# Transposed x in one tile per supergroup, and another pace of the x loads, in an attention and MLP kernel

## Chip, cores and metric

The kernel runs on 1 core of one Trainium2 chip. The metric is the device time of one execution in microseconds (us); the median over runs counts. Below, PE is TensorE, ACT ScalarE, DVE VectorE, POOL GpSimd and SP SyncE. POOL and SP issue the DMAs here; each issues in the order of its own queue, so an issue that waits holds back all that stand behind it.

## The reference

Four batches of 12480 tokens with 128 channels pass through an attention with 32 inducing points, and the result through an MLP of width 2048 with a leaky activation.

```python
def _attn_ref(x, inducing):            # x (4, 12480, 128), inducing (32, 128)
    def mab(q, kv):
        s = scale * (q @ kv.transpose(0, 2, 1))
        s = s - s.max(-1, keepdims=True)
        a = np.exp(s)
        a /= a.sum(-1, keepdims=True) + 1e-09
        return a @ kv
    h = mab(I, x)                      # 32 rows per batch
    return mab(x, h)

def _moe_ref(x, w_in, w_out, alpha):   # w_in (128, 2048), w_out (2048, 128)
    h = x @ w_in
    g = np.maximum(h, 0.0) + alpha * np.minimum(h, 0.0)
    return g @ w_out
```

Each batch therefore needs its x twice: once in full for `h`, and then again for the scores of each token against `h`. Nothing of a batch's second half can start before all of its x has been seen.

## The kernel before

**Tiling.** A batch is six supergroups of 2048 tokens and a rest of 192. A supergroup is four groups of 512 tokens, so a batch has 25 groups (the last one is the rest), and groups are numbered through: batch 0 has 0 to 24, batch 1 has 25 to 49, and so on. A full group is worked in four slots, j 0 to 3; the rest in two. (g, j) below names a slot. There are 392 slots.

**One slot.** `fill` multiplies the softmax numerators of the group (`rep`, the 32 rows of a group copied to four blocks of partitions) by `hW` (which is `h` times `w_in`): four matmuls that write four of six PSUM banks (`ring`). ACT and DVE empty these banks through a ReLU into `gt`; a planner (`make_plan`, a beam search over estimated costs) decides beforehand which of the two takes which bank. After the fill come the tasks that are registered for the slot, then up to two POOL "moves", and then `mm2` of the slot before: four matmuls `acc<-gt,W` with `w_out` scaled by one minus alpha. The linear part of the activation is added by small matmuls (`hA`). In slots with a task that writes 32 output columns per matmul (scores and sums), `mm2` is written as 16 narrow matmuls in place of four wide ones.

**Output.** From the second supergroup of batch 0 on, the result comes out with channels on partitions. `turn` transposes 32x32 blocks on DVE into `yT`; the last group of a supergroup appends 20 moves: 16 shuffles `yq<-yT` (DMAs issued by POOL), and four times a multiplication by the reciprocal of the softmax denominators (`ob`, on POOL) with the DMA of the result. Two moves go out per slot, four at the end of the last batch.

**x.** For batch 0 a prologue loads and transposes x with PE. For the batches 1 to 3 this is done beside the slots of the batch before:

- `a_load` (POOL): 2048 tokens from DRAM into `xn`, cast to bf16, seven such tiles in rotation; the rest goes to `xnr`. The load is made to wait for the ACT instruction last recorded, so that it does not start before its slot.
- `a_xpose` (SP): a DMA transpose `xT<-xn`, one group later.
- `a_scores`: PE multiplies the inducing points by `xT`, ACT takes the exponential `e1`, SP transposes that by DMA into `e1T`.
- `a_accum`: PE multiplies `e1T` by `xn`; DVE adds the result to `hacc`.
- When all seven pieces are in, `h_sum`, `h_den`, `h_transpose`, `h_weights` and `h_linear` make `h`, `hW` and `hA`.
- `b_scores(s)`: PE multiplies `h` by `xT` of supergroup s, ACT takes the exponential, SP writes it to DRAM (`e2d<-e`). One group later `b_rep` reads it back with four SP DMAs (`rep<-e2d`), one for each block of 32 partitions. `b_den` makes the reciprocal of the denominators.

`xT` is one tile for a whole batch, in two buffers that alternate.

**Order.** Each instruction recorded through `pin` keeps its place in the program on its engine. `at(slot, fn, j)` registers a task; the loop from line 818 gives the groups. For each batch it registers first the `b_scores` and `b_rep` of its supergroups, and then the x work for the batch after it; where two tasks share a slot, the one registered first goes first. For the first supergroup of batch 1, `b_scores` stands in slot (21, 1) and `b_rep` in (22, 0); its first fill is in (25, 0). For the batches 2 and 3 the same two come one group earlier before the change of batch. For the rest of batch 0, `b_scores` is in (18, 3) and `b_rep` in (19, 3).

The tuples in the x part (lines 832 to 846) hold, for the seven pieces in the order 0, 1, rest, 2, 3, 4, 5, the group of the load (`k`), of the scores (`t`) and, as a distance from `t`, of the sum (`d`).

Of the kernel before, what the change touches and what calls it, by code (L numbers as in the profile page):

```python
# [16 lines left out]
P = 128  # L17
NB = 4
GRP = P * NB
NQ = 4  # L20
# [5 lines left out]
def kernel(  # L26
# [11 lines left out]
    bf16 = mybir.dt.bfloat16  # L38

    B, N, C = x.shape  # L40
# [3 lines left out]
    NS = N // SUP  # L44
    REM = N - NS * SUP
    JR = 2
    PR = REM // JR
    assert REM == PR * JR and 0 < PR <= 96 and PR % 16 == 0, REM
    NG = NS * NQ + 1
# [22 lines left out]
    const = ctx.enter_context(tc.tile_pool(name="const", bufs=1))  # L72
    work = ctx.enter_context(tc.tile_pool(name="work", bufs=2))
    xn_pool = ctx.enter_context(tc.tile_pool(name="xnp", bufs=7))
    xt_pool = ctx.enter_context(tc.tile_pool(name="xtp", bufs=2))
    gt_pool = ctx.enter_context(tc.tile_pool(name="gtp", bufs=4))
    head_pool = ctx.enter_context(tc.tile_pool(name="headp", bufs=3))
    rep_pool = ctx.enter_context(tc.tile_pool(name="repp", bufs=3))
# [21 lines left out]
    def mm(o, lhsT, rhs, start=True, stop=True, **kw):  # L100
        return pin(nc.tensor.matmul(o, lhsT, rhs, start=start, stop=stop, **kw))  # L101
# [5 lines left out]
    def new_batch(b):  # L107
        st = Batch()
        st.b = b
        st.xT = xt_pool.tile([C, NS, NQ, GRP], bf16, name="xT", tag="xT")  # L110
        st.xTr = xt_pool.tile([C, JR, PR], bf16, name="xTr", tag="xTr")
        st.xn = {}
        st.e1T = {}
        st.sc = scale
        st.rs = None
        st.e2 = {}
        st.d = {}
        st.rep = {}
        st.rden = {}
        st.yT = {}  # L120
        if b > 0:
            st.es = work.tile([P, NS + 1], f32, name="es", tag="es")
            st.hacc = work.tile([P, C], f32, name="hacc", tag="hacc")
            nc.vector.memset(st.es[:], 0.0)
            nc.vector.memset(st.hacc[:], 0.0)
        return st

    def a_load(st, u, pieces=1):
        t0 = u * SUP
# [26 lines left out]

    def a_xpose(st, u):
        xn = st.xn[u]
        if u < NS:
            pin(nc.sync.dma_start_transpose(  # L160
                out=st.xT[:, u, :, :].rearrange("c q (j p) -> c (q j) p", j=NB),
                in_=xn[:].rearrange("p q f -> p (q f)"),
            ))
        else:
            pin(nc.sync.dma_start_transpose(
                out=st.xTr[:], in_=xn[:].rearrange("p j c -> p (j c)")
            ))


    def p_xpose(st, u, i, last=False):  # L170
        xn = st.xn[u]
        if u == NS:
            tp = bank()[:].bitcast(bf16)
            for j in range(JR):
                pin(nc.tensor.transpose(
                    tp[:, j * PR : (j + 1) * PR], xn[:, j, :], ident[:PR, :PR]
                ))
            pin(nc.vector.tensor_copy(
                out=st.xTr[:].rearrange("c j p -> c (j p)"), in_=tp[:, :REM]
            ))  # L180
            return
        cut = 2 if last else 1
        for h in range(cut):
            tp = bank()[:].bitcast(bf16)
            qs = range(2 * i + h * 2 // cut, 2 * i + (h + 1) * 2 // cut)
            for n, q in enumerate(qs):
                for j in range(NB):
                    k = n * NB + j
                    pin(nc.tensor.transpose(  # L189
                        tp[:, k * P : (k + 1) * P], xn[:, q, j * C : (j + 1) * C], ident[:]  # L190
                    ))
            dst = st.xT[:, u, qs[0] : qs[-1] + 1, :].rearrange("c q t -> c (q t)")
            w = len(qs) * GRP
            if h == 0:
                pin(nc.vector.tensor_copy(out=dst, in_=tp[:, :w]))  # L195
            else:
                pin(nc.scalar.copy(out=dst, in_=tp[:, :w]))

    def p_blocks(st, u, i):
        if u == NS:  # L200
            return [(st.xTr[:, j, :], st.xn[u][:, j, :]) for j in range(JR)]
        return [
            (st.xT[:, u, q, j * P : (j + 1) * P], st.xn[u][:, q, j * C : (j + 1) * C])
            for q in (2 * i, 2 * i + 1) for j in range(NB)
        ]

# [32 lines left out]
    def warm(st, n=1, a=0):  # L239
        for _ in range(n):  # L240
            mm(
                accs[a][:, 1:, :].rearrange("p k c -> p (k c)"), ident[:],
                st.xT[:, 0, 0, : 3 * P], start=False, stop=False, skip_group_check=True,
            )

    def p_sums(st):
# [33 lines left out]
    def a_scores(st, u):  # L280
        ps = bank()
        if u < NS:
            for q in range(NQ):
                mm(ps[32 * q : 32 * q + 32, :], IT[:], st.xT[:, u, q, :])
            e1 = e1_pool.tile([P, GRP], bf16, name="e1", tag="e1")
            pin(nc.scalar.activation(  # L286
                out=e1[:], in_=ps[:], func=EXP, scale=scale, accum_out=st.es[:, u : u + 1]
            ))
            e1T = e1_pool.tile([P, NB, P], bf16, name="e1T", tag="e1T")
            pin(nc.sync.dma_start_transpose(out=e1T[:], in_=e1[:]))  # L290
        else:
            mm(ps[0:M, :REM], IT[:], st.xTr[:].rearrange("c j p -> c (j p)"))
            pin(nc.scalar.activation(
                out=e1r[:, :, :PR],
                in_=ps[0:M, :REM].rearrange("m (j p) -> m j p", j=JR),
                func=EXP, scale=scale, accum_out=st.es[0:M, u : u + 1],
            ))
            e1T = work.tile([P, JR, M], bf16, name="e1Tr", tag="e1Tr")
            pin(nc.sync.dma_start_transpose(
                out=e1T[:], in_=e1r[:].rearrange("m j p -> m (j p)")  # L300
            ))
        st.e1T[u] = e1T
# [69 lines left out]
    def b_scores(st, s):  # L372
        ps = bank()
        if s < NS:
            for q in range(NQ):
                mm(ps[32 * q : 32 * q + 32, :], st.hT, st.xT[:, s, q, :])
            e2 = work.tile([P, GRP], bf16, name="e2", tag="e2")
            pin(nc.scalar.activation(out=e2[:], in_=ps[:], func=EXP, scale=scale_of(st)))  # L378
            w = GRP
        else:  # L380
            mm(ps[0:M, :REM], st.hT, st.xTr[:].rearrange("c j p -> c (j p)"))
            e2 = work.tile([M, REM], bf16, name="e2r", tag="e2r")
            pin(nc.scalar.activation(out=e2[:], in_=ps[0:M, :REM], func=EXP, scale=scale_of(st, M)))
            w = REM

        nq = NQ if s < NS else 1
        st.d[s] = dram.tile([32 * nq, w], bf16, name="e2d", tag="e2d" if s < NS else "e2dr")
        pin(nc.sync.dma_start(out=st.d[s][:], in_=e2[:]))
        st.e2[s] = e2
# [11 lines left out]
    def b_scores_pe(st, q):  # L401
        if q == 0:
            st.rep0 = rep_pool.tile([P, NQ, GRP], bf16, name="rep", tag="rep")
        ps = bank()
        mm(ps[:], st.hT4[:], st.xT[:, 0, q, :])
        pin(nc.scalar.activation(
            out=st.rep0[:, q, :], in_=ps[:], func=EXP, scale=scale_of(st)
        ))
        st.rep[q] = st.rep0[:, q, :]
# [254 lines left out]
    order = [0, 1, NS] + list(range(2, NS))  # L664
    st = new_batch(0)
# [94 lines left out]

    pool = accs[0][:, 0, :M]
    den = accs[1][:, 0, 0:1]
    halves = [(u, i) for u in order for i in range(1 if u == NS else 2)]
    n = len(halves)
    p_xpose(st, *halves[0])
# [30 lines left out]
    states = {0: st}  # L796
# [4 lines left out]
    def at(slot, fn, j=1, cost=None, narrow=False):  # L801
        tasks.setdefault((slot, j), []).append((fn, cost))
        if narrow:
            narrows.add((slot, j))
# [10 lines left out]
    at(2, late_finish, 0)  # L815
    at(2, lambda: linear(st, [1]), 0)

    for b in range(B):
        base = b * NG
        for s in range(1, NS + 1):  # L820
# [5 lines left out]
        if b + 1 < B:  # L826
# [3 lines left out]
                states[n] = new_batch(n)  # L830

            for i, u in enumerate(order):
                if b == 0:
                    k, t = (1, 3, 4, 6, 8, 10, 12)[i], (6, 7, 9, 11, 13, 15, 17)[i]
                    d = (4, 4, 4, 4, 4, 3, 2)[i]
                    turn_at = k + 1, 1
                else:
                    k, t = base + (-8, -6, -4, -3, 0, 3, 6)[i], base + (-3, -1, 1, 3, 6, 9, 12)[i]
                    d = (4, 5, 4, 5, 5, 4, 5)[i]
                    turn_at = k + 1, 1 if k + 1 == base - 1 else 3  # L840
                if i == 0:
                    at(k, begin)
                at(k, lambda n=n, u=u: a_load(states[n], u), 3 if i == b == 0 else 1)
                at(turn_at[0], lambda n=n, u=u: a_xpose(states[n], u), turn_at[1])
                at(t, lambda n=n, u=u: a_scores(states[n], u), 0, (215, "A", 680), narrow=True)
                at(t + d, lambda n=n, u=u: a_accum(states[n], u), 3, (200, "D", 220), narrow=True)
            k = base + NG - (6 if b == 0 else 7)
            at(k, lambda n=n: h_sum(states[n]), 0)
            at(k, lambda n=n: h_den(states[n]), 1, (250, "D", 500))
# [126 lines left out]
```

## Time and profile before

| | us |
|---|---|
| median of 11 runs | 587.93 |
| lowest and highest of them | 585.61, 593.45 |
| the profiled execution | 583.84 |
| its span in the profile | 582.1 |
| PE busy | 567.1 |
| ACT busy | 511.5 |
| DVE busy | 507.0 |
| POOL busy (its DMA issues counted) | 358.3 |

The median is that of whole executions. The span is the time from the first to the last instruction in the profile, and lies inside the profiled execution's own time. Busy times are sums over the span; a matmul's end is modelled, so PE's busy time holds some waiting. The views used below are: the page (busy times, the chain of work that ended last, DMA issues with the median time from issue to landing), the timelines of one engine (start, time taken, engine, line, operation, count, and in brackets the idle time before it with what ended it), and the waits (engine and line, what it waited for, total us, times, longest).

```text
PE   4999999999999999999999999999999999999997
POOL 6631056385674758775756576687674876766761
DMA  9959699977899499555799869854353454444333
```

These three rows cut the span into 40 slices of 14.6 us; a digit is the busy share in tenths. The last ten slices or so belong to the last batch, which has no x to load for a next one.

### The profile page before, as it was taken

The page shows a single profiled execution, that of the slowest core. Times are in us where ns is not written, and L with a number is a line of the kernel's source. Part 1 is how long each engine was busy: PE and PEld are TensorE (multiplying, and loading weights), DVE is VectorE, ACT ScalarE, POOL GpSimd, SP SyncE. Part 2 cuts the span into 40 slices and gives each one's busy share as a digit, 9 for nine tenths or more (in the row PEclk, how much of TensorE's full clock was granted, in tenths as well). Part 3 has the DMA queues.
Part 4 walks back from the last instruction along what each step waited for, and adds up shares of the span by engine and source line. Part 5 has one row for each costly group of instructions (what it writes and reads, how often), then busy time and mean ns, then how long its engine had stood idle before and what let it go on. Part 6 is the DMA issues. An engine that isn't in the chain of part 4 may idle for free.

```text
span 582.1 us, 14829 instructions
## 1 busy us (share of the span) xinstructions
PE 567.1 (97%) x5491; PEld 224.6 (39%) x5491; DVE 507.0 (87%) x851; ACT 511.5 (88%) x1010; POOL 358.3 (62%) x614
## 2 busy tenths in 40 slices
PE   4999999999999999999999999999999999999997
PEld 4675333333333333333333333333333333333375
DVE  3689998888988998898898989889899999999995
ACT  2588999998889999998989989999898999999986
POOL 6631056385674758775756576687674876766761
PEclk9999999999999999999999999999999999999999
DMA  9959699977899499555799869854353454444333
GB/s 198 216 108 205 119 178 196 186 160 145 171 240 196 122 200 217 160 163 111 165 193 211 182 136 218 177 149 149 99 155 114 131 127 140 128 113 141 112 107 135
DMA packets 94104, 92.75 MB, mean 159 GB/s; under 512 B 61984, under 2 KB 77520, under 8 KB 94032
## 3 DMA queue, kind: packets, MB, share of 16 engines
q0 software_dynamic: 24016, 60.29, 43.6%
q1 hardware_dynamic: 69872, 30.99, 25.5%
q8 instruction: 43, 0.70, 0.6%
q10 hardware_dynamic: 144, 0.52, 0.3%
q14 instruction: 29, 0.24, 0.2%
HBM read 40.20 MB, written 28.75 MB: 118 GB/s over the span
## 4 chain that ended last, share of the span: by engine, by line
PE 91%; ACT 3%; DMA 2%; DVE 2%; issue 1%; SPq 0%; DVEq 0%
PE acc L101 62%; PE ring L101 28%; ACT gt L485 3%; PE ring L189 1%; DVE gt L487 1%; DMA rep<-e2d 1%; DMA ind_f<-in_inducing_dram 1%; DMA e2d<-e 1%; DVE xT L195 0%; DVE rdt L424 0%; SPq L396 0%; DVE xn L757 0%; ACT e L378 0%; SPq L669 0%; DVE ind_b L707 0%
## 5 line engine op out<-in xcount | busy, mean ns | idle before, releaser
L485 ACT ACTIVATE gt<-ring 128x512 bf16<-128x512 f32 (+1 forms) x921 | 480.2, 600 | 50.3 <-ACT gt L485 28.1
L487 DVE TENSOR_SCALAR gt<-ring 128x512 bf16<-128x512 f32 x647 | 418.3, 682 | 51.7 <-PE ring L101 41.8
L101 PE MATMUL acc<-gt,W 128*32 128x512 bf16 (+2 forms) x2272 | 370.6, 377 | 0.0
L631 POOL DMA_DIRECT2D yq<-yT x352 | 173.3, 500 | 70.5 <-DMA xn<-in_x_dram 27.2
L101 PEld LDWEIGHTS <-W 128*128 128x128 bf16 (+1 forms) x2272 | 122.3, 97 | 147.6 <-issue 63.0
L101 PE MATMUL ring<-rep,hW 32*128 32x512 bf16 (+1 forms) x1600 | 165.3, 378 | 0.5 <-DMA rep<-e2d 0.2
L638 POOL TENSOR_TENSOR ob<-yq,rd 128x512 f32<-128x512 f32 x88 | 92.7, 1055 | 59.4 <-DMA yq<-yT 58.0
L101 PEld LDWEIGHTS <-hW 32*128 32x128 bf16 x1600 | 44.2, 91 | 158.1 <-issue 151.4
L649 POOL DMA_DIRECT2D out_dram<-ob x84 | 49.2, 585 | 27.9 <-POOL ob L638 24.6
L622 DVE STREAM_TRANSPOSE yT<-acc 128x512 f32<-128x512 f32 x88 | 62.3, 708 | 4.6 <-PE acc L101 4.6
L135 POOL DMA_DIRECT2D xn<-in_x_dram x28 | 15.8, 567 | 34.8 <-ACT gt L485 30.6
L101 PE MATMUL acc<-W,gt 128*128 128x128 bf16 (+1 forms) x544 | 36.1, 220 | 0.0
L101 PEld LDWEIGHTS <-gt 128*128 128x128 bf16 (+1 forms) x544 | 30.7, 99 | 5.7 <-issue 5.1
L101 PE MATMUL acc<-rep,hA 32*128 32x512 bf16 (+1 forms) x91 | 17.4, 371 | 0.0
L214 ACT ACTIVATE e1t<-ring 128x256 bf16<-128x256 f32 (+1 forms) x13 | 4.8, 372 | 10.6 <-PE ring L101 10.5
L195 DVE COPY xT<-ring 128x1024 bf16<-128x1024 bf16 (+1 forms) x12 | 7.9, 669 | 5.0 <-PE ring L189 4.6
L378 ACT ACTIVATE e<-ring 128x512 bf16<-128x512 f32 x18 | 11.0, 614 | 0.0
L286 ACT ACTIVATE e<-ring 128x512 bf16<-128x512 f32 x18 | 10.9, 603 | 0.0
L101 PE MATMUL ring<-xT,hT 128*32 128x512 bf16 (+1 forms) x98 | 10.3, 387 | 0.4
L189 PE MATMUL ring<-ident,xn 128*128 128x128 bf16 x96 | 8.8, 249 | 0.9 <-DVE xn L757 0.9
L593 POOL DMA_DIRECT2D out_dram<-obe x4 | 2.2, 548 | 11.7 <-DVE obe L580 11.7
L101 PEld LDWEIGHTS <-hT 128*32 128x32 bf16 (+1 forms) x122 | 4.6, 93 | 11.2 <-issue 10.7
(102 smaller groups left out, 160.3 us busy)
## 6 DMA issues: line engine op xcount, KB each, us to landing
yq<-yT POOLq DMA_DIRECT2D x352, 64.0 KB, 3.4
out_dram<-ob POOLq DMA_DIRECT2D x84, 256.0 KB, 2.9
rep<-e2d SPq DMA_DIRECT2D x92, 128.0 KB, 3.5
xn<-in_x_dram POOLq DMA_DIRECT2D x18, 512.0 KB, 6.8
e2d<-e SPq DMA_DIRECT2D x24, 128.0 KB, 3.1
xn<-in_x_dram POOLq DMA_DIRECT2D x10, 256.0 KB, 8.5
w_out_f<-in_moe_w_out_dram POOLq DMA_DIRECT2D x4, 256.0 KB, 11.2
out_dram<-obe POOLq DMA_DIRECT2D x4, 256.0 KB, 5.7
```

The costliest lines, as they stand in the source:

```text
L101: return pin(nc.tensor.matmul(o, lhsT, rhs, start=start, stop=stop, **kw))
L135: bi = pin(nc.gpsimd.dma_start(out=xn[:, i * w : (i + 1) * w, :], in_=src[:, i * w : (i + 1) * w, :]))
L189: pin(nc.tensor.transpose(tp[:, k * P : (k + 1) * P], xn[:, q, j * C : (j + 1) * C], ident[:]))
L195: pin(nc.vector.tensor_copy(out=dst, in_=tp[:, :w]))
L286: pin(nc.scalar.activation(out=e1[:], in_=ps[:], func=EXP, scale=scale, accum_out=st.es[:, u : u + 1]))
L378: pin(nc.scalar.activation(out=e2[:], in_=ps[:], func=EXP, scale=scale_of(st)))
L485: pin(nc.scalar.activation(out=gt[:, r, :w], in_=ps[:, :w], func=RELU))
L487: pin(nc.vector.tensor_relu(gt[:, r, :w], ps[:, :w]))
L622: pin(nc.vector.transpose(out=yT[:, :, q, :, :].rearrange("p a j c -> p j a c"), in_=acc[:].rearrange("p j (a c) -> p j a c", a=4),))
L631: pin(nc.gpsimd.dma_start(out=yq[32 * a : 32 * a + 32, k], in_=yT[32 * k : 32 * k + 32, a]))
L638: pin(nc.gpsimd.tensor_tensor(out=ob[:].rearrange("p j (k c) -> p j k c", k=4), in0=yq[:, :, q].rearrange("p k j c -> p j k c"), in1=bass. ...
L649: pin((nc.sync if ending else nc.gpsimd).dma_start(out=out[t0 : t0 + SUP, :].rearrange("(p q j) c -> q p j c", q=NQ, j=NB)[q], in_=ob[:],))
```

## The change

Three things change. The transposed x becomes one tile per supergroup, of which twelve rotate (24 KB per partition and batch before, the same bytes after), and the rest's tile gets three buffers; a tile is now taken when its transpose is issued (`new_xT` in `a_xpose`), not when the batch begins. The places of loads, scores and sums come from a table `PACE` with one row for each batch, counted from the batch's first group; the sum's place is now given itself and not as a distance. And for batch 1 the transposes move from j 1 to j 3 of their group.

```diff
-    xt_pool = ctx.enter_context(tc.tile_pool(name="xtp", bufs=2))
+    xt_pool = ctx.enter_context(tc.tile_pool(name="xtp", bufs=12))
...
-        st.xT = xt_pool.tile([C, NS, NQ, GRP], bf16, name="xT", tag="xT")
-        st.xTr = xt_pool.tile([C, JR, PR], bf16, name="xTr", tag="xTr")
+        st.xT = {}
...
+    def new_xT(st, u):
+        if u < NS:
+            st.xT[u] = xt_pool.tile([C, NQ, GRP], bf16, name="xT", tag="xT")
+        else:
+            st.xTr = xt_pool.tile([C, JR, PR], bf16, name="xTr", tag="xTr", bufs=3)
...
     def a_xpose(st, u):
         xn = st.xn[u]
+        new_xT(st, u)
...
-                mm(ps[32 * q : 32 * q + 32, :], st.hT, st.xT[:, s, q, :])
+                mm(ps[32 * q : 32 * q + 32, :], st.hT, st.xT[s][:, q, :])
...
+    PACE = [
+        [(1, 3, 4, 6, 8, 10, 12), (6, 7, 9, 11, 13, 15, 17), (10, 11, 13, 15, 17, 18, 19)],
+        [(-12, -9, -8, -6, -3, 0, 4), (-6, -3, -1, 0, 3, 7, 11), (0, 1, 4, 5, 8, 12, 16)],
+        [(-17, -13, -12, -9, -5, -1, 4), (-11, -7, -5, -3, 1, 5, 11), (-8, -4, 0, 1, 5, 9, 16)],
+    ]
     for b in range(B):
         base = b * NG
...
             for i, u in enumerate(order):
-                if b == 0:
-                    k, t = (1, 3, 4, 6, 8, 10, 12)[i], (6, 7, 9, 11, 13, 15, 17)[i]
-                    d = (4, 4, 4, 4, 4, 3, 2)[i]
-                    turn_at = k + 1, 1
-                else:
-                    k, t = base + (-8, -6, -4, -3, 0, 3, 6)[i], base + (-3, -1, 1, 3, 6, 9, 12)[i]
-                    d = (4, 5, 4, 5, 5, 4, 5)[i]
-                    turn_at = k + 1, 1 if k + 1 == base - 1 else 3
+                k, t, d = (base + v[i] for v in PACE[b])
+                turn_at = k + 1, 1 if (k + 1) % NG == NG - 1 else 3
...
-                at(t + d, lambda n=n, u=u: a_accum(states[n], u), 3, (200, "D", 220), narrow=True)
+                at(d, lambda n=n, u=u: a_accum(states[n], u), 3, (200, "D", 220), narrow=True)
```

Row b of `PACE` is for the loads of batch b + 1. In group numbers, the loads of batch 2 were posted in the groups 17, 19, 21 (rest), 22, 25, 28 and 31, and are now posted in 13, 16, 17 (rest), 19, 22, 25 and 29. Those of batch 3 were in 42, 44, 46 (rest), 47, 50, 53 and 56, and are now in 33, 37, 38 (rest), 41, 45, 49 and 54. Those of batch 1 stay where they were. All are posted at j 1, but for the very first, at j 3.

More of the change, by code (lines that the diff above doesn't have):

```diff
@@ L158, in a_xpose @@
         xn = st.xn[u]
+        new_xT(st, u)
         if u < NS:
             pin(nc.sync.dma_start_transpose(
-                out=st.xT[:, u, :, :].rearrange("c q (j p) -> c (q j) p", j=NB),
+                out=st.xT[u][:].rearrange("c q (j p) -> c (q j) p", j=NB),
                 in_=xn[:].rearrange("p q f -> p (q f)"),
@@ L191, in p_xpose @@
                     ))
-            dst = st.xT[:, u, qs[0] : qs[-1] + 1, :].rearrange("c q t -> c (q t)")
+            dst = st.xT[u][:, qs[0] : qs[-1] + 1, :].rearrange("c q t -> c (q t)")
             w = len(qs) * GRP
@@ L202, in p_blocks @@
         return [
-            (st.xT[:, u, q, j * P : (j + 1) * P], st.xn[u][:, q, j * C : (j + 1) * C])
+            (st.xT[u][:, q, j * P : (j + 1) * P], st.xn[u][:, q, j * C : (j + 1) * C])
             for q in (2 * i, 2 * i + 1) for j in range(NB)
@@ L242, in warm @@
                 accs[a][:, 1:, :].rearrange("p k c -> p (k c)"), ident[:],
-                st.xT[:, 0, 0, : 3 * P], start=False, stop=False, skip_group_check=True,
+                st.xT[0][:, 0, : 3 * P], start=False, stop=False, skip_group_check=True,
             )
@@ L283, in a_scores @@
             for q in range(NQ):
-                mm(ps[32 * q : 32 * q + 32, :], IT[:], st.xT[:, u, q, :])
+                mm(ps[32 * q : 32 * q + 32, :], IT[:], st.xT[u][:, q, :])
             e1 = e1_pool.tile([P, GRP], bf16, name="e1", tag="e1")
@@ L404, in b_scores_pe @@
         ps = bank()
-        mm(ps[:], st.hT4[:], st.xT[:, 0, q, :])
+        mm(ps[:], st.hT4[:], st.xT[0][:, q, :])
         pin(nc.scalar.activation(
@@ L762 @@
     den = accs[1][:, 0, 0:1]
+    for u in order:
+        new_xT(st, u)
     halves = [(u, i) for u in order for i in range(1 if u == NS else 2)]
```

## Prediction

> **What bounds the kernel now.** I read the page first: its busy row, the chain of waits and the table of DMA issues.
>
> ```profile
> span 582.1 us, 14829 instructions
> PE 91%; ACT 3%; DMA 2%; DVE 2%; issue 1%; SPq 0%; DVEq 0%
> xn<-in_x_dram POOLq DMA_DIRECT2D x18, 512.0 KB, 6.8
> ```
>
> TensorE (PE) sets the end almost alone. I cut its timeline into slots, one per fill (four matmuls `ring<-rep,hW`): a plain slot takes 1.30 us (fills at 159.99 and 161.29). Only one of the 392 slots stands out by more than half a microsecond against slots of the same content: group 25, j 0, the first fill of the second batch. PE's timeline there:
>
> ```profile
> 166.87 1.35 PE L101 MATMUL ring<-rep,hW 32*128 32x512 bf16 x3
> 168.38 0.39 PE L101 MATMUL ring<-rep,hW 32*128 32x512 bf16 x1 [0.16 <-DMA rep<-e2d]
> 168.70 0.83 PE L101 MATMUL acc<-gt,W 128*128 128x192 bf16 x8
> ```
>
> The slot runs from 166.87 to 169.46, 2.59 us; the same slot of the next two batches takes 1.09. So 1.50 us are lost, to the last `rep` of batch 1. Why it is late stands in SP's timeline (the column after the start is how long the issue took):
>
> ```profile
> 154.35 2.28 SPq L160 DMA_TRANSPOSE xT<-xn  x1
> 156.73 1.05 SPq L388 DMA_DIRECT2D e2d<-e  x1
> 161.54 2.08 SPq L396 DMA_DIRECT2D rep<-e2d  x4
> ```
>
> ScalarE had finished that `e` at 150.01 (start 149.37, 0.64 long), but `e2d` left at 156.73, 6.72 late: the x transpose stands ahead of it on SP and waits for its load. The view of waits of the SP queue has this wait 13 times:
>
> ```profile
> SPq L388 <- ACT e L378: 146.6, 16, 18.0
> SPq L160 <- DMA xn<-in_x_dram: 75.2, 13, 15.6
> ```
>
> That load was posted in slot (19, 1), which began at 135.53, and left POOL at 147.18. POOL's timeline says why:
>
> ```profile
> 97.80 0.54 POOL L135 DMA_DIRECT2D xn<-in_x_dram  x1
> ...
> 124.36 3.94 POOL L631 DMA_DIRECT2D yq<-yT  x8
> 128.50 0.57 POOL L135 DMA_DIRECT2D xn<-in_x_dram  x1 [0.20 <-issue]
> 129.32 3.45 POOL L631 DMA_DIRECT2D yq<-yT  x7 [0.24 <-DMA yq<-yT]
> 134.78 0.50 POOL L631 DMA_DIRECT2D yq<-yT  x1 [2.02 <-DMA xn<-in_x_dram]
> 139.37 1.04 POOL L638 TENSOR_TENSOR ob<-yq,rd 128x512 f32<-128x512 f32 x1 [4.09 <-DMA yq<-yT]
> ...
> 147.18 0.55 POOL L135 DMA_DIRECT2D xn<-in_x_dram  x1
> 147.71 3.46 POOL L631 DMA_DIRECT2D yq<-yT  x7
> 154.61 0.50 POOL L631 DMA_DIRECT2D yq<-yT  x1 [3.44 <-DMA xn<-in_x_dram]
> ```
>
> A load costs POOL more than its issue: the eighth DMA after it waits until it has landed (2.02, 3.44), and the shuffles behind it land late (4.09 before the first `ob`). POOL's waits between 97 and 165 us hold none for a slot and none for `yT`: it works off a backlog there. So it has no slack to hide one more load in. Without loads a supergroup is cheap, as in batch 3:
>
> ```profile
> 469.87 7.87 POOL L631 DMA_DIRECT2D yq<-yT  x16 [1.84 <-DVE yT L622]
> 479.86 1.04 POOL L638 TENSOR_TENSOR ob<-yq,rd 128x512 f32<-128x512 f32 x1 [2.13 <-DMA yq<-yT]
> ...
> 487.11 0.58 POOL L649 DMA_DIRECT2D out_dram<-ob  x1 [0.30 <-POOL ob L638]
> ```
>
> 469.87 to 487.69 is 17.82 us; with one load (124.36 to 147.18) it is 22.82.
>
> **The change, part by part.**
>
> *Twelve tiles for two.* The same bytes; a transpose now waits for the readers of one supergroup, not of a batch. The waits of the SP queue show at most two short ones that PE ended before a transpose (4.5 us in sum), while SP sits 146.6 us waiting for ScalarE. I take 0; if that cover were gone, the shorter waits would be worth up to those 4.5.
>
> *Batch 1's transposes from j 1 to j 3 of the same group*: two slots, 2.6 us later on SP, behind that group's `rep` and not ahead of it. The nearest deadline is that of the 192-token piece, turned at (5, 3) and read by PE at (9, 0): 13 slots, about 17 us, against a landing of 4.6 (median). I take 0. Without this cover PE would wait at the scores, by at most the 2.6 us.
>
> *Scores and sums on other slots.* Instruction counts stay, but for one set of narrow second matmuls (16 of 32 columns) that becomes four wide ones; both sets take 1.04 us in PE's timeline. The planner splits the evictions anew; PE waits for a bank 2.3 us in the whole span (ScalarE's row), which bounds this to about -2 to +2. I take 0. The gaps from score to sum grow to 6 groups at first, some 33 us, longer than any `e1T` landing (8.75 at most).
>
> *Loads of batch 2* go from groups 17, 19, 21, 22, 25, 28, 31 to 13, 16, 17, 19, 22, 25, 29. The SP order at the critical place stays: a transpose at (20, 3), then `e2d` at (21, 1), then the four `rep` at (22, 0). Its load is again the one posted at (19, 1). What changes is the POOL queue in front of it: since the load at 97.80 there was one load (128.50); now there are two, and the 48 KB `xnr`. All of POOL's later work moves by their cost, and every link behind the load moves with it: 147.18 to 154.35 (load, 7.17), to 156.73 (transpose issue, 2.38), to 161.54 (`e2d`, 4.81), to 163.20 (fourth issue, 1.66), to 168.33 (landing, 5.13). PE has no slack left there, so the stall grows one for one.
>
> Price of the added load: 22.82 - 17.82 = 5.0, one load against none. Of `xnr`: its issue, 0.66. Sum 5.7. From below: 147.18 to 171.40 holds the same shuffles and outputs with two loads and `xnr` and takes 24.22, which is 1.40 more than with one load. From above: 97.80 to 124.36 took 26.56 with one load, 8.74 over the unloaded, plus 0.66 and the 0.64 that a shuffle waited after `xnr`: 10.0. I take 5.7, since the row with one load against none is the cleanest, and keep 1.4 and 10.0.
>
> The row for the landing is 7.17. The Trainium skill (DMA: Bandwidth & Descriptors, section Anatomy of one DMA, SWDGE path) gives about 2.0 us plus bytes over 436 GB/s; for 1 MB of float32 read that makes an estimate of 4.4. By it the stall of before would not exist and that of after would be 4.4 instead of 7.2.
>
> The same page (section Issuing engines are not separate DMA queues) says that all issuers share 16 DMA engines, and that a sequencer's issue time is usually small beside the transfer. By its second half the two added issues would cost 0.57 + 0.66 = 1.2; the wait rows above speak against that half. The first half speaks against moving loads among the shuffles.
>
> *Loads of batch 3* go from groups 42 to 56 to 33 to 54. At the second batch change `e2d` left at 284.61, ahead of the transpose (292.18), its `rep` went out at 294.49, and PE needed it at about 307: 8 us of margin, no stall to win. I take 0; an extra 5 us there would still be covered.
>
> Sum: 583.84 + 5.7 = 589.5 for an execution like the profiled one. That one lies 4.09 below the median of the runs, so on the median 587.93 + 5.7 = **593.6**; with the bounds, 589.3 to 597.9.
>
> **Rivals.**
>
> *The boundary is relieved (faster).* `xnr`, posted at (21, 1) before, is out of the way, and an earlier first load could be paid while POOL still waits for its slots (11.30 us at 74.99 in the view by time). If the load of (19, 1) leaves POOL 1.5 us earlier than 147.18 or more, the stall is gone: 587.93 - 1.50 = 586.4, and 582.3 if the 4.09 above the profile are the same wait. Against it: POOL's slack is before 97.80, the added load comes after it.
>
> *Absorbed (no change).* The load at (13, 1) runs in the wait for `out_dram` (2.3 us in that window) and `yq`, so that the shift is at its lower end or below: 587.9 to 589.3.
>
> *Twice.* The new transpose at (17, 3) also blocks the `e2d` of the last 192 tokens, at (18, 3), and a second fill waits (group 24, due at 164.27). Its `rep` went out at 138.9, 25 us early, so that takes more than the upper bound: over 598.
>
> *The change does not do what it says*: the seven `xn` tiles could hold the early loads back. Each waits for a sum five groups or more earlier; priced at 0.
>
> **How the numbers follow.** Forecast (a shift of 1.4 to 10.0) 0.70; relieved 0.16; absorbed 0.10; twice 0.04. Half a per cent, 2.9 us, is what a measurement of this kernel tells from no change. Of the forecast about 0.08 lies under that, of relieved 0.04: faster 0.12, same 0.22, slower 0.66. The range cuts the ends of relieved and twice: 585 to 599.
>
> **What would show it.** In the profile after: the load before the blocked transpose leaves POOL some 5 us later against slot (19, 1), with two waits on `xn` loads between the groups 13 and 19; SP issues that transpose, `e2d` and `rep` later by as much; the fill of group 25 waits 5 to 10 us; the other batch changes are clean. I am wrong if that load leaves within 12 us of its slot, or if the fill waits no longer than now.

## The result, and the profile after

| | before | after |
|---|---|---|
| median of the runs, us | 588.28 (48 runs) | 592.89 (13 runs) |
| lowest and highest, us | 582.11, 594.62 | 590.63, 596.45 |
| the profiled execution, us | 583.84 | 592.89 |
| its span, us | 582.1 | 591.0 |

The ratio of after to before is 1.0099, with the interval [1.0075, 1.0123]: slower by 1%, which is 5.8 us on 588.28. The ratios here compare undisturbed runs round by round, so they are not exactly the quotients of the medians beside them.

The profiles lie 8.9 us apart, more than the medians. Cut into the same 392 slots as in the prediction, before lost 12.0 us in all against the shortest slots of the same content, and after 19.2. The starts of the slots say where: after is 0.3 us later at (19, 1), 0.3 earlier at (24, 1), 7.2 us later at (25, 0), 9.4 at (50, 0) and 9.0 at the last slot. So nearly all of it comes in one place: 7.46 us are lost ahead of the first fill of the second batch, and 3.2 more in the slots (25, 0) and (25, 1), against the same two slots in e5 below, where PE does not wait. (Slot (25, 0) of after holds scores too and has no second of its kind in that profile, so the 19.2 do not hold its loss.) In all the place costs after 10.7 us, and before 1.50.

The page of after, its first line, the shares of the chain that ended last, two groups and one DMA issue (the last columns of a group: busy us, mean ns, idle us before them and what ended most of it):

```profile
span 591.0 us, 14799 instructions
...
PE 90%; DMA 5%; DVE 2%; ACT 2%; issue 1%; SPq 0%; DVEq 0%
...
L637 POOL DMA_DIRECT2D yq<-yT x352 | 172.8, 500 | 84.1 <-DMA xn<-in_x_dram 39.9
...
L101 PE MATMUL ring<-rep,hW 32*128 32x512 bf16 (+1 forms) x1600 | 165.3, 379 | 7.6 <-DMA rep<-e2d 7.4
...
xn<-in_x_dram POOLq DMA_DIRECT2D x18, 512.0 KB, 6.6
```

DMA has 5% of the chain where it had 2%. The fills waited 7.4 us for `rep` (0.2 before). POOL's shuffles waited 39.9 us for x loads, where they had waited 27.2, although the number of loads is the same and their median landing nearly so (6.6, before 6.8). The lines of after's file are some six further down than before's: L631 is L637, L160 is L166, L388 is L394, L396 is L402.

PE's timeline of after at the batch change (the third line is from a narrower view and shows the fourth of the four fills alone; lines in between are left out):

```profile
165.80 0.83 PE L101 MATMUL acc<-gt,W 128*128 128x192 bf16 x8
174.03 2.42 PE L101 MATMUL ring<-rep,hW 32*128 32x512 bf16 x4 [7.39 <-DMA rep<-e2d]
175.84 0.60 PE L101 MATMUL ring<-rep,hW 32*128 32x512 bf16 x1
...
178.32 0.61 PE L101 MATMUL ring<-rep,hW 32*128 32x512 bf16 x4
...
180.13 0.40 PE L101 MATMUL ring<-rep,hW 32*128 32x512 bf16 x4
```

The same stretch cut into windows (from and to, length, PE's busy time and its instructions, the granted clock of TensorE as a share of full speed; the last two columns are of the DMAs):

```profile
160.00:166.00 6.00, 5.90 (x77) 1.00 1.15 112
166.00:174.00 8.00, 0.64 (x8) 0.70 0.97 201
174.00:178.00 4.00, 3.85 (x15) 0.50 1.20 251
178.00:180.00 2.00, 2.00 (x11) 0.62 1.18 288
180.00:190.00 10.00, 9.91 (x115) 1.00 1.12 221
```

The first `rep` holds PE until 174.03, and the other three, which land one after the other, until 175.84. During the wait the granted clock falls to 0.50, and it is back at 1.00 only by 180: four fills take 0.61 us at 178.32 and 0.40 at 180.13. In before's profile the clock is 1.000 over the whole span. So PE loses time after the wait too. Without the wait PE would have been at these fills at 166.6 (slot (24, 1) begins at 165.45 and takes 1.12 in e5); some 9.3 of the 10.7 us lie ahead of the fourth fill, and some 1.4 behind it.

The chain of waits of after there (start, us, what):

```profile
163.98 0.06 ACT e L384
164.04 5.00 DMA e2d<-e
169.04 0.02 issue
169.05 0.32 SPq L402
169.37 0.04 issue
169.41 5.25 DMA rep<-e2d
```

The chain reaches PE's second fill at 174.71 over `rep` and `e2d`. Its first link here is not the true one: the activation that ends at 164.47 and that it names belongs to the next supergroup, while the `e` that this `e2d` writes was ready at 149.86 (ACT's timeline: 149.21, 0.65 long). SP was busy elsewhere until 164.00. SP's own timeline shows with what (the second column is how long the issue took; the last line, from a narrower view, is the fourth `rep` alone):

```profile
159.69 4.31 SPq L166 DMA_TRANSPOSE xT<-xn  x1
164.04 0.59 SPq L394 DMA_DIRECT2D e2d<-e  x1
169.05 1.74 SPq L402 DMA_DIRECT2D rep<-e2d  x4
170.36 0.43 SPq L402 DMA_DIRECT2D rep<-e2d  x1
```

The same three as before, in the same order: 154.35, 156.73 and 161.54 there. The transpose is issued 5.34 us later, and takes 4.31 where it took 2.28, so `e2d` is 7.31 later and the first `rep` 7.51. The fourth `rep` lands 5.4 after its issue, at 175.79, where it was 168.33. The waits of SP's queue:

```profile
SPq L166 <- DMA xn<-in_x_dram: 129.8, 15, 14.7
```

Transposes that stand at the head of SP's queue and wait for their load have gone from 75.2 us to 129.8. That holds for the whole kernel and not for one place. POOL's timeline of after, between the loads in question:

```profile
106.53 0.57 POOL L140 DMA_DIRECT2D xn<-in_x_dram  x1
107.10 3.43 POOL L637 DMA_DIRECT2D yq<-yT  x7
116.55 0.50 POOL L637 DMA_DIRECT2D yq<-yT  x1 [6.02 <-DMA xn<-in_x_dram]
...
127.56 0.56 POOL L140 DMA_DIRECT2D xn<-in_x_dram  x1
128.09 3.45 POOL L637 DMA_DIRECT2D yq<-yT  x7
134.74 0.50 POOL L637 DMA_DIRECT2D yq<-yT  x1 [3.19 <-DMA xn<-in_x_dram]
135.24 0.65 POOL L147 DMA_DIRECT2D xnr<-in_x_dram  x1
141.52 0.50 POOL L637 DMA_DIRECT2D yq<-yT  x1 [0.84 <-DMA xnr<-in_x_dram]
...
153.03 0.56 POOL L140 DMA_DIRECT2D xn<-in_x_dram  x1
```

Two loads (106.53, 127.56) and `xnr` now stand ahead of the load that was posted in slot (19, 1), and the eighth DMA behind each waits for its landing (6.02, 3.19, 0.84). That load leaves at 153.03, 17.2 us behind its slot, where it left 11.7 behind.

How far each load leaves POOL behind the start of the slot it is posted in (POOL's timeline against PE's slots, us; the six x loads of batch 2, then the six of batch 3, in order; for loads that an experiment moved, behind the slot that they have in after; the kernels are those of the experiments):

| kernel | loads of batch 2 | loads of batch 3 |
|---|---|---|
| before | 4.6, 11.7, 6.5, 3.9, 14.7, 10.1 | 2.3, 8.2, 4.4, 4.7, 14.4, 10.4 |
| after | 5.4, 9.2, 17.2, 13.9, 2.6, 5.5 | 7.5, 10.1, 12.9, 14.5, 17.1, 17.8 |
| e1, batch 2's old places | 5.1, 11.6, 5.6, 2.4, 15.5, 10.8 | 11.5, 19.7, 20.5, 18.3, 20.0, 17.3 |
| e2, batch 3's old places | 6.4, 9.6, 16.4, 11.4, 2.6, 5.0 | 2.3, 8.7, 5.0, 5.4, 14.4, 9.7 |
| e3, after, `rep` ahead | 5.4, 9.3, 16.7, 14.6, 10.5, 16.4 | 16.7, 18.5, 20.1, 16.6, 19.0, 19.0 |
| e10, after, two loads ahead | 6.3, 10.6, 7.6, 9.2, 8.6, 11.9 | 13.6, 15.0, 18.7, 6.7, 16.8, 19.1 |

This table was not part of the prediction, and it is the one that orders what follows. In after the lag drops from 13.9 to 2.6 at the fifth load: PE's wait of 7.5 us before it has let POOL catch up.

### The profile page after: what moved, and what is told of

The parts are those of the page before. It is cut to its first block, busy times and chain, and to the rows that moved or that the text cites. A ratio compares the mean times of both kernels' runs of the same rounds, so it can differ in the third digit from the quotient of the medians.

```text
span 591.0 us, 14799 instructions
## 1 busy us (share of the span) xinstructions
PE 568.6 (96%) x5479; PEld 224.6 (38%) x5479; DVE 505.8 (86%) x850; ACT 512.9 (87%) x1011; POOL 357.2 (60%) x614
## 4 chain that ended last, share of the span: by engine, by line
PE 90%; DMA 5%; DVE 2%; ACT 2%; issue 1%; SPq 0%; DVEq 0%
PE acc L101 61%; PE ring L101 27%; ACT gt L491 2%; DMA xT<-xn 2%; DMA xn<-in_x_dram 1%; PE ring L195 1%; DVE gt L493 1%; DMA rep<-e2d 1%; DMA ind_f<-in_inducing_dram 1%; DMA e2d<-e 1%; DVE xT L201 0%; DVE yT L628 0%; DVE xn L763 0%; DVE hW L276 0%; SPq L675 0%
## 5 line engine op out<-in xcount | busy, mean ns | idle before, releaser
L637 POOL DMA_DIRECT2D yq<-yT x352 | 172.8, 500 | 84.1 <-DMA xn<-in_x_dram 39.9
L101 PEld LDWEIGHTS <-W 128*32 128x32 bf16 (+1 forms) x2260 | 122.8, 97 | 147.6 <-issue 63.5
L655 POOL DMA_DIRECT2D out_dram<-ob x84 | 49.0, 584 | 25.0 <-POOL ob L644 24.7
L101 PE MATMUL ring<-xT,hT 128*32 128x512 bf16 (+1 forms) x98 | 10.4, 387 | 0.5
L599 POOL DMA_DIRECT2D out_dram<-obe x4 | 2.2, 547 | 11.7 <-DVE obe L586 11.7
L101 PEld LDWEIGHTS <-hT 128*32 128x32 bf16 (+1 forms) x122 | 4.6, 93 | 11.6 <-issue 11.1
## 6 DMA issues: line engine op xcount, KB each, us to landing
w_out_f<-in_moe_w_out_dram POOLq DMA_DIRECT2D x4, 256.0 KB, 10.7
```

The source lines that it names most:

```text
L637: pin(nc.gpsimd.dma_start(out=yq[32 * a : 32 * a + 32, k], in_=yT[32 * k : 32 * k + 32, a]))
L655: pin((nc.sync if ending else nc.gpsimd).dma_start(out=out[t0 : t0 + SUP, :].rearrange("(p q j) c -> q p j c", q=NQ, j=NB)[q], in_=ob[:],))
```

## The experiments

The theory: POOL works off a backlog, the added loads lengthen it, the late load holds a transpose at the head of SP's queue, and `e2d` and `rep` behind it come too late. The rival that the runs were to exclude says that the DMA engines are simply fuller, so that the order on POOL and SP does not matter; and a second one that the tiles or j 3 cost something. Each run was timed beside runs of before on the same chip, and the ratios are to those.

**e1: after, with batch 2's loads, scores and sums in their old places.** What is left of the change is batch 3's part, the tiles and j 3.

```diff
-        [(-12, -9, -8, -6, -3, 0, 4), (-6, -3, -1, 0, 3, 7, 11), (0, 1, 4, 5, 8, 12, 16)],
+        [(-8, -6, -4, -3, 0, 3, 6), (-3, -1, 1, 3, 6, 9, 12), (1, 4, 5, 8, 11, 13, 17)],
```

> After, with the pace of batch 2 as it was before (loads in the groups 17, 19, 21, 22, 25, 28, 31); twelve tiles, j 3 and the new pace of batch 3 stay. POOL theory: two posts fewer stand in front of the load of slot (19, 1), so the first fill of batch 1 waits some 1.5 us as before and not 7.5, and the time is 586 to 590. Rival, the cost lies in the tiles, in j 3 or in batch 3's pace: the fill may be on time, but the time stays at 591 to 595.

Measured: 592.33 median (10 runs), ratio 1.0062 [1.0005, 1.0120]. In its profile (593.79) 1.53 us are lost at group 25, as in before, but new waits stand further on: 2.65 at (42, 3), which has no twin to be measured against, 4.55 lost at (51, 0), and under one each at (39, 0), (43, 3) and (46, 3). PE's timeline at the two large ones:

```profile
271.91 0.41 PE L101 MATMUL ring<-xn,e1T 128*32 128x128 bf16 x16 [2.65 <-DMA e1T<-e]
...
322.07 0.62 PE L101 MATMUL ring<-xT,IT 128*32 128x512 bf16 x4 [3.42 <-DMA xT<-xn]
```

SP's timeline of the same run before the first, and POOL's load that its transpose waits for:

```profile
263.27 3.07 SPq L166 DMA_TRANSPOSE xT<-xn  x1
266.44 1.46 SPq L296 DMA_TRANSPOSE e1T<-e  x1
```

```profile
256.76 0.55 POOL L140 DMA_DIRECT2D xn<-in_x_dram  x1
```

The time is the rival's, not the theory's: batch 3's places are not free, though the interval only just leaves out 1. The load left POOL 19.7 us behind its slot, its transpose went out when it had landed (263.27), and the `e1T` that stood behind it on SP reached the sum too late. The same queue, another victim: first a sum, then, at (51, 0), the scores themselves.

**e2: after, with batch 3's places old.** The same row of numbers in the third line of `PACE`.

> After, with the pace of batch 3 as it was before (loads in the groups 42 to 56). POOL theory: the 7.5 us before group 25 stay, and only the wait of the scores in group 51 (1.0 us) goes, so 591 to 594. Rival, batch 3's pace costs the time: 588 or less.

Measured: 593.82 (4 runs), ratio 1.0130 [1.0060, 1.0200]. The profile (590.94) loses 4.70 us ahead of the first fill of group 25, 3.15 in that slot against the same one in e5, and 1.07 and 0.61 in the next two (the granted clock is 0.50 here too, to 179.7), and none over a third of a microsecond from there to the end, but the 0.50 at (48, 0) that before has too. So batch 2's part alone makes the loss at the batch change, and the waits of e1 belong to batch 3's part. The two look as if they did not add up (1.3% and 0.6% alone, 1.0% together), but their intervals are too wide to show it.

**e3: after, with the one transpose at group 20 turned behind the `rep`.** Only SP's order changes.

```diff
+                if (b, k) == (1, 19):
+                    turn_at = 22, 1
```

> After, with one transpose moved on SP: that of the load of slot (19, 1) goes from (20, 3) to (22, 1), behind the e2d and the rep of batch 1's first supergroup. No DMA is added or taken away, POOL's queue is the same. POOL and SP theory: the load is as late as in after (some 17 us behind its slot), but e2d and rep no longer wait for it; the 7.5 us fall to 0 to 2 (the scores in group 25 then wait for the transpose), so 585 to 588. Rival, the DMA engines are too busy there for rep to arrive in time, whatever the order: 591 to 594.

Measured: 592.91 (10 runs), ratio 1.0111 [1.0068, 1.0155]. In its profile (589.37) the fills of group 25 begin at 165.9 with no wait, with POOL's load as late as in after (16.7 behind its slot); the scores in the same slot then wait 1.98 for that transpose. So the place is what the theory says: it is SP's order, and not the DMA traffic, that makes `rep` late. The time was not won (585 to 588 was expected): 3.71 us are lost at (42, 3), 0.70 and 0.99 in the next group and 1.98 at (51, 0). The table shows why: without the 7.5 us at (25, 0) the lag of the fifth load is 10.5 and not 2.6, and that of the load whose transpose stands ahead of (42, 3)'s `e1T` is 18.5 and not 10.1. PE's wait in after was also POOL's slack.

**e4: the same line in before.**

> Before, with the same one transpose moved from (20, 3) to (22, 1). Theory: its 1.5 us at the first fill of batch 1 go, in an execution like the profiled one; as the runs lie some 4 us over that one, and if this wait is what differs from run to run, up to 5 us go: 583 to 587. Rival, the runs differ by something else: 586 to 588.

Measured: 590.46 (4 runs), ratio 1.0101 [1.0018, 1.0184]: slower, where faster was expected. PE's timeline, SP's timeline and the chain of waits of its profile:

```profile
168.58 0.62 PE L101 MATMUL ring<-xT,IT 128*32 128x512 bf16 x4 [3.95 <-DMA xT<-xn]
```

```profile
150.05 0.34 SPq L388 DMA_DIRECT2D e2d<-e  x1
152.75 1.74 SPq L396 DMA_DIRECT2D rep<-e2d  x4
155.94 7.85 SPq L160 DMA_TRANSPOSE xT<-xn  x1
```

```profile
155.94 12.60 DMA xT<-xn
```

`e2d` leaves at once when its `e` is there (150.05; ACT has it ready at 150.02), and group 25 is nearly clean; but the transpose now has a deadline of its own, the scores at (24, 0), and it went out 0.15 us after the next x load (155.79). PE lost 5.08 us at (24, 0) and 0.86 behind it. The transpose's issue took 7.85 us and it landed after 12.60, where the median of that group of transposes in before is 6.3. In e3 the same transpose has more room, since its scores stand one group later there, at (25, 0).

**e5: after, with the load of slot (19, 1) posted one group earlier**, at (18, 1). In POOL's queue it then stands ahead of four `ob` and their outputs, and not behind them; the loads, their number and their bytes are after's.

```diff
-                at(k, lambda n=n, u=u: a_load(states[n], u), 3 if i == b == 0 else 1)
+                at(18 if (b, k) == (1, 19) else k, lambda n=n, u=u: a_load(states[n], u), 3 if i == b == 0 else 1)
```

> After, with one load moved on POOL: the one of slot (19, 1) is posted in (18, 1), ahead of the four ob of its supergroup and not behind them (4 times 1.96 us). SP's order and every DMA stay. POOL theory: the load leaves about 7.8 us earlier, its transpose too, e2d and rep follow, and the 7.46 us before group 25 fall to 0 to 1.5. In the two runs where that wait was short, batch 3's pace made new ones in the groups 39, 42 and 51 (together 5 to 10 us in the profile), so I expect those here, and a time of 589 to 594. Rival, rep is late from busy DMA engines and not from the order on POOL: 5 us or more stay before group 25.

Measured: 586.79 (10 runs), ratio 0.9985 [0.9952, 1.0017], some two microseconds better than the range expected. POOL's, SP's and PE's timelines of its profile (586.67):

```profile
143.57 0.57 POOL L140 DMA_DIRECT2D xn<-in_x_dram  x1 [0.20 <-ACT gt L491]
145.49 1.04 POOL L644 TENSOR_TENSOR ob<-yq,rd 128x512 f32<-128x512 f32 x1 [1.35 <-DMA yq<-yT]
```

```profile
150.20 2.66 SPq L166 DMA_TRANSPOSE xT<-xn  x1
152.91 1.56 SPq L394 DMA_DIRECT2D e2d<-e  x1
158.31 2.87 SPq L402 DMA_DIRECT2D rep<-e2d  x4
```

```profile
167.10 0.40 PE L101 MATMUL ring<-rep,hW 32*128 32x512 bf16 x4
...
168.53 0.57 PE L101 MATMUL ring<-rep,hW 32*128 32x512 bf16 x4
...
170.00 0.39 PE L101 MATMUL ring<-rep,hW 32*128 32x512 bf16 x4
```

The load leaves 9.5 us earlier than in after, everything behind it follows, and group 25 does not wait: its first two slots take 2.90 us, and 6.10 in after (174.03 to 180.13). One item moved in one queue takes the whole loss of the change away, with the same traffic; that excludes the fuller DMA engines as the cause of the large wait. Left are 3.38, 1.07 and 0.41 us from (51, 0) on, batch 3's part.

**e7: before, with that load moved in the same way.**

> Before, with the same load moved from (19, 1) to (18, 1). Theory: the 1.5 us at the first fill of batch 1 go and nothing new comes, since the loads of batch 3 lie late as before: 582 to 586. If the runs of before differ by this wait, their spread shrinks too. Rival, the earlier load delays ob and the next loads as much as it gains: 587 to 590.

Measured: 585.82 (10 runs), ratio 0.9954 [0.9909, 0.9999]. In its profile (589.07) group 25 is clean, and (49, 0) loses 6.11 us to scores that wait for their `xT`. That execution is slower than the median, so it is likely that this wait comes and goes.

**e8 and e8b: after with batch 3's old places (e2) and the load moved (e5), both.** The same kernel, timed on two occasions.

> After, with batch 3's pace as before and the load of (19, 1) posted in (18, 1). If batch 2's new pace costs only through this one late load, the 4.7 us and the 1.7 behind it that the run with batch 3's old pace showed around group 25 fall under 1.5, and the time is 584 to 588. If the added load and the rest's load make POOL late in general, other waits come around the change of batch: 589 to 593.

> The version with the new pace of batch 2, the old pace of batch 3 and the load of (19, 1) ahead of the ob, once more and with more rounds: 580 to 585, faster than both kernels. It says whether the four runs of before were a lucky draw.

Measured: 580.99 (4 runs), ratio 0.9884 [0.9824, 0.9944], and 582.27 (12 runs), ratio 0.9955 [0.9910, 1.0000]. Profiles of 580.90 and 581.52, with no slot that loses over half a microsecond. POOL's load and SP's timeline of e8b:

```profile
143.02 0.57 POOL L140 DMA_DIRECT2D xn<-in_x_dram  x1 [0.19 <-ACT gt L491]
```

```profile
149.07 2.56 SPq L166 DMA_TRANSPOSE xT<-xn  x1
151.67 0.69 SPq L394 DMA_DIRECT2D e2d<-e  x1
155.48 1.78 SPq L402 DMA_DIRECT2D rep<-e2d  x4
```

The last `rep` is issued by 157.26, and PE fills at 166.25. This version has the lowest median of all, some 6 us under before (587.97 beside it) and 10 under after; the second interval touches 1, so that it beats before is likely, by half to one per cent, and not beyond doubt. Against e5, which differs in batch 3's places alone and was timed in the same session, e8 shows again what those places cost once the large wait is gone: 586.79 and 580.99.

**e9: after, with the places of both batches old.** What is left is the twelve tiles and j 3 of batch 1's transposes.

> After, with the pace of both batches as before: only the twelve tiles and the two slots later for batch 1's transposes are left of the change. Both were taken as 0: 586 to 589, with some 1.5 us at the first fill of batch 1. Rival, the tiles change the waits of the transposes: outside of that.

Measured: 589.55 (582.24 to 596.69, 10 runs), ratio 0.9966 [0.9915, 1.0017]: no cost that can be told from none, though the median of all ten lies 2.3 above that of before beside it. Its profile (590.85) loses 0.50 at (25, 0), 1.20 at (29, 0), 4.97 at (34, 0) and 1.14 at (49, 0). The last two are scores that wait for their `xT`, at (34, 0) behind a load that left POOL 23.0 behind its slot, in a kernel with the old places; the one at (29, 0) is a wait for a bank.

**e10: after, with two loads moved**, that of (19, 1) to (18, 1) and that of (45, 1) to (43, 1).

> After, with two loads ahead of the four ob of their supergroup: that of slot (19, 1) in (18, 1), as in the run above, and that of (45, 1) in (43, 1). In that run the scores of group 51 still waited 3.4 us and 1.5 behind it, for a transpose whose load left POOL about 15 us behind its slot. If this is the one place where batch 3's pace costs, it goes and the time is 580 to 584; if POOL is late in general, another wait comes: 585 to 588.

Measured: 583.01 (12 runs), ratio 0.9951 [0.9914, 0.9989]. In its profile (583.06) groups 25 and 51 are clean; 1.09 at (42, 3) and 0.83 at (43, 3) are left. The lag of the moved loads is 7.6 and 6.7. So batch 3's new places can be kept too, if the load with the nearest deadline goes ahead of the `ob`.

**e11: before, unchanged, a second profile.**

> The kernel before once more, for a second profiled execution. The one shown lost 1.5 us at group 25 and lies 4 us under the median. If the runs of before differ by the same kind of wait (a transpose whose load left POOL late, with PE waiting for scores or rep behind it) this execution shows such waits, at group 25 or near the groups 29, 34 and 49, whose sum explains its time within 1.5 us. If they differ by something else (clock, evictions), the slots show an even loss.

Measured: 587.78 (8 runs), ratio 1.0026 [0.9970, 1.0082]. The profile (586.88, span 585.1) has group 25 clean: the load left at 144.19, three microseconds earlier than in the first profile. Instead (49, 0) loses 3.73 us and (49, 1) 0.87. The two profiles differ by 3.0 us in span and by 3.1 in these waits (4.60 against 1.50). So before's runs differ, at least in part, in where and whether a wait of this kind falls.

**e6: after, with batch 2's rest (`xnr`) back at (21, 1)**, where it was before, so that only the added x load stands ahead of the critical one.

```diff
+                if (b, u) == (1, NS):
+                    k, turn_at, t, d = 21, (22, 3), 26, 30
```

> After, with the 192-token rest of batch 2 loaded, turned, scored and summed as before ((21, 1), (22, 3), group 26, group 30). It leaves one load, not a load and the 48 KB rest, as what was added in front of the load of slot (19, 1). By the sum of the prediction the load makes 5.0 of the shift and the rest 0.7, so that load leaves POOL some 5 us later than in before and 0.7 earlier than in after, and 6 to 7 us stay before group 25. If the rest's row is worth more (its issue, 1.36 and 0.84 of waits behind it), 2.5 to 3 us go.

Measured: 594.77 (2 runs), ratio 1.0145 [1.0042, 1.0247]. 8.15 us are lost ahead of the first fill of group 25. POOL's and PE's timelines:

```profile
154.19 0.55 POOL L140 DMA_DIRECT2D xn<-in_x_dram  x1
```

```profile
174.62 2.35 PE L101 MATMUL ring<-rep,hW 32*128 32x512 bf16 x4 [8.08 <-DMA rep<-e2d]
```

The load leaves no earlier than in after (154.19 against 153.03), where 0.7 earlier was expected. What `xnr` costs in that place can't be told from this: the load's lag differs by three microseconds between two profiles of one kernel (before and e11).

## Why the prediction was right, and where not

*Direction, place and mechanism: right.* The loss stands at the first fill of group 25, and each link is there. The load left 5.85 us later (5.7 predicted), the transpose was issued 5.34 later, `e2d` 7.31 and the first `rep` 7.51. e3 shows SP's part and e5 POOL's by changing nothing but the order on the one or the other. The two waits on `xn` loads that were to stand between the groups 13 and 19 are the 6.02 and 3.19.

*The sum of 5.7: right as a sum, with its terms unsettled.* The supergroup with the added load took 29.73 us (97.83 to 127.56), against 26.56 for the one of before that began at the same time: 3.2, not 5.0. The next took 25.47 (127.56 to 153.03) against 22.82: 2.65 with `xnr` in it, not 0.66. That supergroup already had a load and waits in it, which may be why the second load added only 3.2: the row with none was the cleanest, but not the nearest. That the 2.65 is the price of `xnr` is not shown; e6 without it had a supergroup of 25.0. Two misses in opposite directions left the sum right, and that is luck.

*"One for one": wrong by two microseconds.* The prediction counts the stall up to the last `rep`: 1.50 before, 7.2 after. By that count it was 9.3 (166.6 to 175.84), so 5.85 us at the load became 7.8 at PE. The link that grew is the transpose on SP: its issue took 4.31 us, which the chain of the prediction held at the 2.28 of before. The last link gave nothing back, 6.74 us from the first `rep` issue to the last landing (169.05 to 175.79) for 6.79 (161.54 to 168.33).

*No term for the clock.* The sum ends when the last `rep` lands. In after the granted clock had fallen to 0.50 by then, and PE lost some 1.4 us more before it was back. By the profiles the place grew by 9.2 us (10.7 less 1.50) and not by 5.7.

*Tiles and j 3 at 0: right* (e9, within its interval).

*Loads of batch 3 at 0: wrong.* Alone they cost 0.6% [0.05, 1.2] (e1, just clear of nothing), and e5 against e8 points the same way. The step looked at one consumer, the `e2d` and `rep` of the batch change, and its margin of 8 us was indeed enough: no fill there waited. But a transpose at SP's head delays whatever stands behind it in the middle of the batch too, and the ones that ran out were `e1T` for a sum at (42, 3) and `xT` for the scores at (51, 0). The size could have been read from the lag table. In before 11 groups without a load lie between batch 2's last load and batch 3's first, and the lag falls from 10.1 to 2.3 there. In after only 4 do, and from then on nearly every supergroup has its load: POOL takes 24.7, 25.0 and 25.0 us from one to the next (231.26, 255.99, 281.02, 306.05), while PE takes 22.1, 22.2 and 23.5 for the same four groups (slots at 223.8, 245.9, 268.1 and 291.6). So the lag grows by some 2 us with each and is never worked off while loads go on. The new places spread the loads; for POOL that is a longer stretch without rest. In after little of it shows ("the other batch changes are clean" missed 1.01 us at (51, 0)), because the 7.5 us at (25, 0) came first. A cost was hidden by the loss beside it, and e3 and e5 lay it open. It is no cost against a clean kernel: with the old places similar waits fell at (49, 0) in e7, e9 and e11.

*From the profile to the median: right by luck.* 5.7 was added to the median, and 4.6 was measured (5.8 by the ratio), where the profiles differ by 8.9. Two misses nearly cancel in the 593.6. The place cost some 3.5 us more than the 5.7, by the transpose's issue and the clock. And before's median already held waits that after's profiled execution, which lies at its own median, hardly shows. The 4.09 between before's profile and its median was perhaps the wait at group 25, by the rival of relief. The runs show waits of that kind, but elsewhere: e11, the second profile, lost 3.73 at (49, 0) and nothing at (25, 0), and e9 and e7, with the old places, lost 4.97 at (34, 0) and 6.11 at (49, 0). The granted clock says how common they are. Of 72 executions of before beside the experiments, all between 582 and 596 us, 26 had a mean clock of 0.999 or more and a median of 583.9, and 46 had less, with a median of 589.3; in every profile here where the clock falls before the kernel's end, it does so at a wait of PE.

*The rivals.* Relief needed the load to leave 1.5 us earlier; it left 5.85 later. Absorbed needed a shift at the lower end. Twice: group 24 did not wait. As for the rule on a DMA's landing that the prediction weighed (the Trainium skill, DMA: Bandwidth & Descriptors, section Anatomy of one DMA), which made an estimate of 4.4 us: the load that matters took 6.66 from its start to the issue of the transpose that waited for it (153.03 to 159.69), 7.17 in before. The measurement decides.

What stays open: how much of batch 2's loss is `xnr`'s, why the issue of the transpose took 4.31 us and not 2.28, and what makes a load of one and the same kernel leave POOL three microseconds earlier in one execution than in another.

## What to carry to other kernels

Price an added item in an in-order queue by how far that queue already lags behind its posting (the lag table, one number per load), and then follow everything that stands behind the late item on the next queue, not only its nearest consumer. An item with a far-reaching consumer goes ahead of work that it does not depend on: here one load moved ahead of four `ob` took away all that the new pace had cost. PE's long waits cost more than their length here, so look at the granted clock behind them. A wait that is removed gives back its time only if nothing used it as slack, so look at what is late next, and where runs spread over 2%, take more than one profile of the same kernel.

## What the runs showed of the hardware

A transpose's issue on SP is no constant: 2.28 us in before, 4.31 in after at the same place, and 7.85 in e4, where it went out 0.15 us behind the next x load, with a landing of 12.60. The eighth DMA behind a load of `xn` on POOL waited between 2.02 and 6.02 us in the lines shown, though the issue of the load itself took 0.54 to 0.57 in all of them. So a load costs POOL far more than its issue, and in these lines the wait varied threefold.

The granted clock fell to 0.50 at PE's long waits in the middle of the kernel: in all ten profiles with a wait of 2.76 us (e3) or more, and at none of the shorter ones, up to 2.65 (e1). It stayed there for 3.41 us in e1, e3, e5, e7, e9 and e11, for 6.83 in e4 (a wait of 3.95), for 10.24 in after and e2, and for 13.65 in e6 (a wait of 8.08).
